# The last unit's stores: upper feature half through GpSimd's queue, lower half in four pieces of 64 KB

## The chip, the cores and the metric

The kernel runs on one core of one Trainium2 chip. The metric is the device time of one execution in microseconds (us). A core has TensorE (PE, matrix products), VectorE (DVE), ScalarE (ACT), GpSimd (POOL) and SyncE (SP); data enters and leaves through 16 DMA engines, which serve queues fed by SP, ACT and POOL.

## The reference

Attention whose keys and values are averaged over groups of 8 rows, followed by a mixer of two layers over tokens and two over channels. Cut to what matters:

```python
# q, k, v: (8 batches, 8 heads, 576 rows, 64)
k_p, v_p = mean of k and v over groups of 8 rows          # 72 rows each
attn_out = softmax(q @ k_p.T / 8) @ v_p
x  = attn_out, heads side by side                          # (8, 576, 512)
h  = relu(x.T @ w_tok1) @ w_tok2                           # over the 576 tokens
u  = x + h.T
out = u + relu(u @ w_ch1) @ w_ch2                          # 512 -> 1536 -> 512, float32
```

## The kernel before, in words

The work is ordered by hand: the whole body runs in a manual schedule. A head (`HEAD`) loads the first data, and then nine units follow, `unit(0)` to `unit(8)`, each with a plan (`PLANS`) of steps of later batches that are set between its own. Units 0 to 7 each take 512 of the 576 rows of one batch through the channel layers. The 64 rows that remain of every batch (the ninth row of each group of nine) are gathered in `u_tails` and `uT_tails`, and unit 8, the last one (`n == B`), takes the 512 rows of all eight batches at once.

From unit 2 on a unit is a `unit_fast`. It splits the second channel product (`GT`, hidden features, by `w_ch2`) into quarters and uses seven products of half size in the manner of Strassen instead of eight, with sums of the blocks in `area` and `area2`. `lo` and `hi` are the lower and the upper 256 of the 512 output features. PE's products are made by `product` (L777), which sums over `NH` = 6 blocks for each of two blocks `i` of 128 rows. The additions that complete an output are made on DVE by `plus` (L799). The outputs are two tiles, `oa` and `ob`, each of 128 partitions x 2 row blocks x 512 float32.

In units 2 to 7 `oa` and `ob` leave by `store` (L580): two issues on SP of 256 KB, one for each half of the partitions. In the last unit `oa` leaves in the same way. The products for `ob` come after it, the upper features first, each with a callback that is called after each row block `i`:

```python
store(n, 0, oa)
...
plus(ob[:, :, hi], x, s5, store_part(hi))
...
plus(ob[:, :, lo], x, u2lo, store_part(lo))
```

`store_part` (L810) does nothing after block 0. After block 1 it stores that feature half of `ob` for both blocks: partitions 0 to 63 by SP's queue and partitions 64 to 127 by ACT's, 128 KB each, as 128 rows of 1 KB. There are four such stores in all. `oa` has rows of 2 KB.

Nothing else is left to do at that point. The last work of POOL (L277, L145) lies near 177 us.

Of the kernel before, what the change touches and what calls it, by code (L numbers as in the profile page):

```python
# [61 lines left out]
def kernel(  # L62
# [14 lines left out]
    nc = tc.nc  # L77
# [4 lines left out]
    BP, BR = 64, S // 64  # L82
# [490 lines left out]
    def store(n, g, o):  # L573
        for half in range(2):
            rows = slice(half * BP, (half + 1) * BP)
            if n == B:
                dst = out.rearrange("(c h) (p r) n -> h p c r n", h=2, r=BR)[half][:, 2 * g:2 * g + 2, 8, :]
            else:
                dst = out[n].rearrange("(p r) n -> p r n", r=BR)[:, 4 * g + half:4 * g + half + 3:2, :]
            nc.sync.dma_start(out=dst, in_=o[rows])  # L580
# [26 lines left out]
    lo, hi = slice(0, 256), slice(256, 512)  # L607
# [30 lines left out]
    def keep(name):  # L638
        return outp.tile([P, 2, 256], FP32, name=name, bufs=1)
# [130 lines left out]
    def unit_fast(n, u):  # L770
        last = n == B
        late_steps = yield from (first_fast if n in GROUPS else first_stage)(n, u)

        def product(ps, a, w, start, after, split=False):
            for i in range(2):
                for m in range(NH):
                    nc.tensor.matmul(out=ps[i] if split else ps[:, i], lhsT=a(m)[:, i * P:(i + 1) * P], rhs=w(m),  # L777
                                     start=start and m == 0 and (i == 0 or split), stop=(m == NH - 1),
                                     skip_group_check=True)
                    if (i * NH + m) % 4 == 3 and (i, m) != (1, NH - 1):  # L780
                        yield
                if split:
                    after(i)
            if not split:
                after(slice(0, 2))
            yield

        def bank(split=False):
            if split:
                return [ps_two.tile([P, 2, 512], FP32, name="p2")[:, 0, 0:256] for _ in range(2)]  # L790
            return ps_one.tile([P, 2, 256], FP32, name="p1")

        def plus(out, ps, other, then=None):
            def go(i):
                src, dst = ps[i] if type(ps) is list else ps[:, i], out[:, i]
                if len(other.shape) == 4:
                    src, dst = (x.rearrange("p (a r) -> p a r", a=4) if type(i) is int else
                                x.rearrange("p c (a r) -> p c a r", a=4) for x in (src, dst))
                nc.vector.tensor_tensor(out=dst, in0=src, in1=other[:, i], op=ALU.add)  # L799
                if then is not None:  # L800
                    then(i)
            return go

        def store_part(cols):
            def go(i):
                if i == 0:
                    return
                for half in range(2):
                    dst = out.rearrange("(c h) (p r) n -> h p c r n", h=2, r=BR)[half]
                    (nc.scalar if half else nc.sync).dma_start(out=dst[:, 2:4, 8, cols],  # L810
                                                               in_=ob[half * BP:(half + 1) * BP, :, cols])
            return go

        SG, TW = fast["S"], fast["T"]

        def half_of(c, k):
            part = u["u"][:, c:c + 2]
            if n < BOUNCED or last:
                return part[:, :, 256 * k:256 * k + 256]
            return part.rearrange("p c (a k r) -> p c k a r", a=4, k=2)[:, :, k]  # L820

        u1lo, u1hi, u2lo, u2hi = half_of(0, 0), half_of(0, 1), half_of(2, 0), half_of(2, 1)
        oa, ob = (outp.tile([P, 2, DM], FP32, name="o") for _ in range(2))
        x, y = bank(last), bank()
        s1 = keep("s1")
        for i, _ in enumerate(product(x, lambda m: GT[:, m, lo], lambda m: w_ch2[:, m, lo], True,
                                      plus(s1, x, u1lo), last)):
            yield
            if late_steps and i < 2:
                late_steps[i]()  # L830
                yield
        yield from product(y, lambda m: GT[:, NH + m, lo], lambda m: w_ch2[:, NH + m, lo], True, plus(oa[:, :, lo], y, s1))
        z = bank()
        s5 = keep("s5")
        yield from product(z, lambda m: SG[:, 0, m], lambda m: TW[:, 0, m], True, plus(s5, z, u2hi))
        s2 = keep("s1")
        yield from product(x, lambda m: SG[:, 1, m], lambda m: TW[:, 1, m], False,
                           plus(s2, x, u1hi), last)
        if not last:
            w = bank()  # L840
            s4 = keep("s4")
            yield from product(w, lambda m: GT[:, NH + m, hi], lambda m: TW[:, 3, m], True, plus(s4, w, u2lo))
        yield from product(z, lambda m: SG[:, 3, m], lambda m: w_ch2[:, NH + m, hi], False, plus(oa[:, :, hi], z, s2))
        store(n, 0, oa)
        if last:
            yield from product(x, lambda m: SG[:, 2, m], lambda m: TW[:, 2, m], False,
                               plus(ob[:, :, hi], x, s5, store_part(hi)), True)
            yield from product(x, lambda m: GT[:, NH + m, hi], lambda m: TW[:, 3, m], False,
                               plus(ob[:, :, lo], x, u2lo, store_part(lo)), True)
        else:  # L850
            def finish(i):
                plus(ob[:, :, hi], x, s5)(i)
                plus(ob[:, :, lo], x, s4)(i)
            yield from product(x, lambda m: SG[:, 2, m], lambda m: TW[:, 2, m], False, finish)
            store(n, 1, ob)
# [112 lines left out]
```

## Time and profile before

| | |
|---|---|
| median of 3 runs | 271.18 us (270.85 to 271.25) |
| profiled execution, its own time | 271.6 us |
| its span, first to last instruction | 269.8 us |
| busy: PE, DVE, ACT, POOL | 96%, 77%, 45%, 42% of the span |
| moved by SP's queue (q1), ACT's (q10), POOL's (q0) | 12.39, 0.33, 22.11 MB |
| granted TensorE clock | 1.000 |

The span is what the trace shows; the time of an execution has 1.8 us more around it. An engine's busy share is a mean over stages, so for a change at the end of the kernel only the rows of the last stage count. A DMA issue's row on SP, ACT or POOL lasts as long as the issuing takes; the data moves later, and "landing" is counted from the start of the issue. The DMA share in a window is the mean busy share of the 16 engines; beside a window's edges it can read a little over 1.

### The profile page before, as it was taken

To read this page: it belongs to the slowest core of one execution; us is meant where nothing else is said; L and a number is where in the kernel's file an instruction comes from. 1 tells how busy PE (TensorE), PEld (TensorE's weight loads), DVE (VectorE), ACT (ScalarE), POOL (GpSimd) and SP (SyncE) were. 2 spreads that over 40 slices of the span, in tenths; PEclk is the share of its full clock that TensorE was granted. 3 is DMA by queue.
4 is the path that set the end of the run, shared out by engine and by line. 5 is a ranking of instruction groups with operands and counts; after the bars stand their busy time and mean duration, and the time that the engine had idled before them with its cause. 6 is when DMAs were issued, how large, how long until landed. Compare 5 with 4: busy or idle time off the path is not lost.

```text
span 269.8 us, 5432 instructions
## 1 busy us (share of the span) xinstructions
PE 259.5 (96%) x2173; PEld 171.7 (64%) x2200; DVE 206.8 (77%) x427; ACT 122.7 (45%) x207; POOL 113.4 (42%) x114
## 2 busy tenths in 40 slices
PE   8999999999999999999999999999999999999992
PEld 2776454545544645776587657864785688787781
DVE  4755573751798859996978798899799889997981
ACT  1375773047444353736563637264922632613600
POOL 5847749999995428636657242420000000000000
PEclk9999999999999999999999999999999999999999
DMA  7999999959969898998995997361506510404106
GB/s 184 190 194 205 204 212 204 180 126 190 153 132 140 154 159 118 146 169 168 155 141 83 156 213 87 39 164 40 119 0 147 149 18 21 137 2 116 41 2 157
DMA packets 42081, 35.17 MB, mean 130 GB/s; under 512 B 12040, under 2 KB 34408, under 8 KB 42056
## 3 DMA queue, kind: packets, MB, share of 16 engines
q0 software_dynamic: 30672, 22.11, 55.3%
q1 hardware_dynamic: 11056, 12.39, 17.2%
q10 hardware_dynamic: 328, 0.33, 0.5%
q8 instruction: 17, 0.28, 0.4%
q14 instruction: 8, 0.07, 0.1%
HBM read 36.90 MB, written 10.49 MB: 176 GB/s over the span
## 4 chain that ended last, share of the span: by engine, by line
PE 90%; DVE 5%; ACT 2%; issue 1%; DVEq 0%
PE p L777 24%; PE p L561 22%; PE p L695 9%; PE p L592 8%; PE p L453 6%; PE p L468 5%; PE p L357 4%; PE p L391 3%; PE p L862 3%; PE p L480 2%; PE p L323 1%; DVE area L614 1%; DVE u L470 1%; ACT ex L379 1%; ACT x L426 1%
## 5 line engine op out<-in xcount | busy, mean ns | idle before, releaser
L564 ACT ACTIVATE GT<-p 128x512 bf16<-128x512 f32 x76 | 44.5, 596 | 57.6 <-PE p L561 43.7
L561 PE MATMUL p<-uT,w_ch 128*128 128x512 bf16 x274 | 69.3, 380 | 0.9 <-issue 0.4
L561 PEld LDWEIGHTS <-w_ch 128*128 128x128 bf16 x304 | 32.4, 114 | 24.1 <-issue 1.7
L362 ACT ACTIVATE ex<-p 72x1024 bf16<-72x1024 f32 (+1 forms) x42 | 31.6, 804 | 27.5 <-PE p L357 27.3
L777 PEld LDWEIGHTS <-area 128*128 128x128 bf16 x336 | 31.9, 98 | 5.3 <-issue 1.3
L777 PE MATMUL p<-area,area 128*128 128x256 bf16 x252 | 30.8, 273 | 0.0
L145 POOL DMA_DIRECT2D kr<-in_k_dram x16 | 23.4, 1495 | 15.6 <-DMA kr<-in_k_dram 15.6
L145 POOL DMA_DIRECT2D vr<-in_v_dram x16 | 23.1, 1478 | 14.2 <-DMA vr<-in_v_dram 14.2
L470 DVE TENSOR_TENSOR u<-p,x 128x512 bf16<-128x512 f32 x32 | 21.1, 680 | 8.2 <-PE p L468 8.2
L777 PEld LDWEIGHTS <-GT 128*128 128x128 bf16 x252 | 24.2, 98 | 4.9 <-issue 0.6
L592 PE MATMUL p<-w_ch,GT 128*128 128x512 bf16 x92 | 23.6, 379 | 0.2
L777 PE MATMUL p<-w_ch,GT 128*128 128x256 bf16 x168 | 20.6, 273 | 0.1
L799 DVE TENSOR_TENSOR o<-p,s 128x512 f32<-128x512 f32 (+1 forms) x28 | 17.9, 662 | 3.2 <-PE p L777 3.1
L396 DVE TENSOR_TENSOR x<-p,den 128x512 bf16<-128x512 f32 x28 | 19.4, 691 | 1.0
L468 PE MATMUL p<-AT,w_tok 128*128 128x512 bf16 x62 | 17.3, 379 | 0.5 <-DVE u L470 0.5
L799 DVE TENSOR_TENSOR s<-p,u 128x512 f32<-128x512 f32 x24 | 16.2, 680 | 2.0 <-PE p L777 2.0
L395 DVE RECIPROCAL den<-p 128x8 f32<-128x8 f32 (+1 forms) x35 | 7.0, 201 | 11.3 <-PE p L391 10.9
L391 PEld LDWEIGHTS <-ex 72*128 72x128 bf16 x280 | 12.6, 98 | 3.9 <-DVE x L396 0.2
L592 PEld LDWEIGHTS <-GT 128*128 128x128 bf16 x96 | 8.8, 98 | 9.4 <-issue 0.4
L453 PE MATMUL p<-x,w_tok 128*128 128x512 bf16 x53 | 13.7, 379 | 0.2
L446 ACT ACTIVATE AT<-p 128x512 bf16<-128x512 f32 x14 | 8.4, 597 | 12.1 <-PE p L453 11.7
L391 PE MATMUL p<-vp,ex 72*128 72x65 bf16 x280 | 13.7, 194 | 0.0
(151 smaller groups left out, 448.8 us busy)
## 6 DMA issues: line engine op xcount, KB each, us to landing
out_dram<-o SPq DMA_DIRECT2D x34, 256.0 KB, 3.8
kr<-in_k_dram POOLq DMA_DIRECT2D x16, 288.0 KB, 7.4
vr<-in_v_dram POOLq DMA_DIRECT2D x16, 288.0 KB, 7.0
qb<-in_q_dram POOLq DMA_DIRECT2D x7, 576.0 KB, 10.1
kr<-in_k_dram POOLq DMA_DIRECT2D x3, 576.0 KB, 10.9
vr<-in_v_dram POOLq DMA_DIRECT2D x3, 576.0 KB, 12.4
w_ch<-in_moe_w_ch_dram POOLq DMA_DIRECT2D x6, 256.0 KB, 10.6
w_ch<-in_moe_w_ch_dram POOLq DMA_DIRECT2D x3, 512.0 KB, 13.1
```

Of the source, the lines that this page charges most:

```text
L145: nc.gpsimd.dma_start(out=pair_sums(b, key), in_=src[:, :, 2 * i * D:2 * (i + 1) * D], accum_op=ALU.add if i else ALU.bypass)
L362: nc.scalar.activation(out=exv[:, a, :, gs[0]:gs[-1] + 1, n0:n0 + n], func=AF.Exp, scale=scale, in_=pss[a][0:SP, :, 0:len(gs) * n].rearran ...
L391: nc.tensor.matmul(out=ps[:, h // 4, (h % 4) * (D + 1):(h % 4 + 1) * (D + 1)], lhsT=st["ex"][:, h * S + n0:h * S + n0 + P], rhs=st["vp"][: ...
L453: nc.tensor.matmul(out=ps, lhsT=w_tok1[:, c if c < 4 else 4 + par, m * P:(m + 1) * P], rhs=st["x"][:, c, :] if c < 4 else st["xt"], start= ...
L468: nc.tensor.matmul(out=ps, lhsT=w, rhs=a, start=(i == 0), stop=(i == len(mms) - 1))
L470: nc.vector.tensor_tensor(out=quads_of(dst, on), in0=plain_of(ps, on), in1=plain_of(x, on), op=ALU.add)
L561: nc.tensor.matmul(out=ps[m], lhsT=w_ch1[m // 4][:, kk, m % 4:512:4], rhs=moving(u)[kk], start=(kk == 0), stop=(kk == 3))
L564: nc.scalar.activation(out=GT[:, m, :], in_=ps[m], func=AF.Relu)
L592: nc.tensor.matmul(out=ps, lhsT=GT[:, m, c * P:(c + 1) * P], rhs=w_ch2[:, m, :], start=(m == 0), stop=(m == NM - 1))
L695: nc.tensor.matmul(out=ps[:, i], lhsT=w(i, k), rhs=mv(k), start=start and (i, k) == (0, 0), stop=stop and k == 1, skip_group_check=True)
L777: nc.tensor.matmul(out=ps[i] if split else ps[:, i], lhsT=a(m)[:, i * P:(i + 1) * P], rhs=w(m), start=start and m == 0 and (i == 0 or spli ...
L799: nc.vector.tensor_tensor(out=dst, in0=src, in1=other[:, i], op=ALU.add)
```

## The change

The callback now acts differently on the two feature halves. For the upper half (`cols == hi`) nothing happens after block 0, as before, and after block 1 both stores of 128 KB are issued from POOL instead of SP and ACT. For the lower half each block is stored as soon as it is complete, so there are two stores of 64 KB after block 0 and two after block 1, on SP and ACT. The bytes and the rows of 1 KB stay the same; L810 becomes L812.

```diff
         def store_part(cols):
             def go(i):
-                if i == 0:
+                if cols == hi and i == 0:
                     return
+                cs = slice(0, 2) if cols == hi else slice(i, i + 1)
                 for half in range(2):
                     dst = out.rearrange("(c h) (p r) n -> h p c r n", h=2, r=BR)[half]
-                    (nc.scalar if half else nc.sync).dma_start(out=dst[:, 2:4, 8, cols],
-                                                               in_=ob[half * BP:(half + 1) * BP, :, cols])
+                    eng = nc.gpsimd if cols == hi else (nc.sync, nc.scalar)[half]
+                    eng.dma_start(out=dst[:, 2 + cs.start:2 + cs.stop, 8, cols],
+                                  in_=ob[half * BP:(half + 1) * BP, cs, cols])
             return go
```

The order of the computing instructions on PE, DVE and ACT is the same in both kernels. POOL has two issues more ahead of its closing instructions.

## The prediction

> **What bounds the kernel now.** I read the chain of waits first, for the last 15 us of the span.
>
> ```profile
> 255.39 9.21 PE p L777 x84
> 264.60 0.02 issue
> 264.62 0.42 DVE o L799
> ```
>
> TensorE (PE) bounds this stage up to the last product, and the last VectorE (DVE) addition follows it at once, ending at 264.62 + 0.42 = 265.04. The span ends at 269.8: 4.8 us at the end have no computation in them. The change touches nothing ahead of 263.7, so everything lies in this tail. Next, the timeline from 261 us on, and what SyncE (SP) waits for in its last line (the columns there: total us, times, longest).
>
> ```profile
> 261.98 1.08 DVE L799 TENSOR_TENSOR o<-p,s 128x512 f32<-128x512 f32 x2 [0.89 <-PE p L777]
> 263.29 0.42 DVE L799 TENSOR_TENSOR o<-p,s 128x256 f32<-128x256 f32 x1 [0.23 <-PE p L777]
> 263.75 2.15 ACTq L810 DMA_DIRECT2D out_dram<-o  x2
> 263.97 0.42 DVE L799 TENSOR_TENSOR o<-p,u_tails 128x256 f32<-128x256 f32 x1 [0.25 <-PE p L777]
> 264.05 1.90 SPq L810 DMA_DIRECT2D out_dram<-o  x2
> 262.70 1.25 SPq L580 DMA_DIRECT2D out_dram<-o  x2
> SPq L963 <- DMA out_dram<-o: 2.4, 3, 1.6
> ```
>
> The upper half of `ob` is complete at 263.29 + 0.42 = 263.71, the first block of the lower half at 263.97 + 0.42 = 264.39, its second block at 265.04. Two stores of `oa` (256 KB each, L580) leave SP from 262.70. SP is still issuing them until 263.95, so its upper-half store starts at 264.05 and ScalarE's (ACT) at 263.75. After that SP waits for landings alone. The rows of L810 (ns min/median/max) and the last issues' landing:
>
> ```profile
> L810 ACTq DMA_DIRECT2D out_dram<-o x2: 738/778/818, 263.7 to 265.1; - x2
> L810 SPq DMA_DIRECT2D out_dram<-o x2: 630/750/870, 264.0 to 265.1; - x2
> DMA to landing us min/median/max: 3.3/3.5/3.7
> ```
>
> Both last issues start at 265.08 (SP's pair ends at 265.95 and the last took 870 ns; ACT's ends at 265.90 and took 818 ns). In the window of that second they land 3.3 us (ACT) and 3.7 us (SP) later, so the last landing is 265.08 + 3.7 = 268.8; another 1.0 us of closing semaphores makes 269.8. Last, what the DMA engines did meanwhile (the last two columns: busy share, GB/s):
>
> ```profile
> 264.00:265.00 1.00, 0.58 (x6) 0.28 (x3) 0.77 (x2) 0.00 (x0) 0.00 (x0) 1.00 0.99 197
> 265.00:266.00 1.00, 0.00 (x0) 0.00 (x0) 0.05 (x1) 0.00 (x0) 0.00 (x0) 1.00 0.96 257
> 265.60:265.80 0.20, 0.00 (x0) 0.00 (x0) 0.00 (x0) 0.00 (x0) 0.00 (x0) 1.00 1.04 317
> 266.40:266.60 0.20, 0.00 (x0) 0.00 (x0) 0.00 (x0) 0.00 (x0) 0.00 (x0) 1.00 0.71 159
> 266.60:266.80 0.20, 0.00 (x0) 0.00 (x0) 0.00 (x0) 0.00 (x0) 0.00 (x0) 1.00 0.77 164
> 267.00:268.00 1.00, 0.00 (x0) 0.00 (x0) 0.00 (x0) 0.00 (x0) 0.00 (x0) 1.00 1.01 285
> 268.30:268.40 0.10, 0.00 (x0) 0.00 (x0) 0.00 (x0) 0.00 (x0) 0.00 (x0) 1.00 0.20 62
> ```
>
> The tail stores 2 x 256 KB + 4 x 128 KB = 1.05 MB. Packets run from 263.9 to 268.36. So the end is set by the drain of the stores and not by the last addition alone. It is not an even drain: while `oa`'s first store runs by itself it moves 197 GB/s, then 317, then there is a dip at 266.4 to 266.8 with the engines 71 to 77% busy, then 285. The queues' packets in slices of 0.2 us say what the dip is: ACT's queue has its first packet of L810 at 265.95, 2.2 us after its issue at 263.75 (SP's first packet of `oa` came 1.2 us after issue), and SP's queue falls there from 31 packets a slice to 10. So the upper half arrives at the engines late, and one store's room is lost.
>
> **The change, part by part.** The profiled execution has a span of 269.8 and a time of 271.6, 1.8 more; the runs' median is 271.18. I carry differences from the span over to the median.
>
> *The upper half leaves SP and ACT.* Two issues go away (630 and 738 ns), with 128 rows of 1 KB each. On SP and ACT nothing stands behind them but the lower half's stores, so this makes both queues free at 264.39: SP has been idle since 263.95. By itself that is worth nothing in issue time, because today both queues are free at 264.68 and 264.49, before 265.04.
>
> *It enters GpSimd's (POOL) queue.* POOL did its last work at 178 us, and behind the two new issues stands only the closing barrier. Their first wait is for the addition ending at 263.71. The trace has no store from POOL, so its price is bounded by the loads:
>
> ```profile
> L180 POOL DMA_DIRECT2D w_tok<-in_moe_w_tok_dram x2: 547/654/762, 2.9 to 24.2; - x2
> L145 POOL DMA_DIRECT2D vr<-in_v_dram x16: 847/1400/2545, 44.5 to 171.0; - x16
> DMA to landing us min/median/max: 5.0/7.1/14.9
> ```
>
> A store here has 128 rows on 64 partitions; L180 has 64 rows, L145 has 576. I take 0.65 us, as the row of nearest shape, and keep 1.4 as the dear end. From 263.75 the two issues then end at 264.4 and 265.05 (dear: 265.15 and 266.55). The load of L145 at 170.96, met by no other traffic, ended its issue at 172.34 and had its first packets at about 172.95, 0.6 us behind. So the upper half's lower partitions reach the engines at about 265.0 and the upper ones at 265.65 (dear: 265.75 and 267.15). With the value taken, that is 0.3 to 1.0 us ahead of the 265.95 of ACT's queue today.
>
> The Trainium skill (DMA: Bandwidth & Descriptors, Latency and other measured facts) gives about 1 us to the first byte on GpSimd's path and 0.6 on the hardware path. By those figures alone the estimate is that the move starts the data 0.4 us later, a loss if the drain follows it; the trace shows both larger (about 2.0 at L145, 1.2 on SP, 2.2 on ACT behind `oa`), so the measured rows decide here.
>
> *The lower half in four stores of 64 KB.* Two issues are added: the first block's start at 264.43 on SP and ACT (ACT started 0.04 us after the addition today). Rows: 630 to 870 ns each, the high end when both queues issue together, so until about 265.25. The second block's issues wait for 265.04, so they start at 265.1 to 265.3 and end by 266.1. Their start is up to 0.2 later than today's 265.08, but they carry 128 KB between them where 256 KB are issued today. Total bytes and rows are unchanged; two more issues mean 32 more completion packets, which I cost at nothing (they are spread on 16 engines; without that cover, two per engine).
>
> *The sum.* Up to 265.2 the trace shows 119 packets of 2 KB, 0.24 MB; 0.805 MB remain. Today they need 268.36 - 265.2 = 3.16 us, a mean of 255 GB/s. With a third queue filled from 265.0, and the first half of the lower columns issued 0.65 us earlier than any of it is today, I expect the dip to go. At 317 GB/s (the slice at 265.6) the rest takes 2.54 us, to 267.74: a gain of 0.62. At 285 (the second at 267) it takes 2.82, to 268.02: 0.34. At the best slice (323 at 267.0) 2.49: 0.67. The last block cannot be what holds this up: from 265.3 with ACT's 3.3 us it would land at 268.6, though that 3.3 covers double the bytes and a full drain. Without that shrinking the gain would end at 0.2, which is the weak end. I take 0.6: span 269.2, its own time 271.0, a median of 270.58, about **270.6**. That case reaches from a gain of 0.2 to one of 1.0: 0.67 by the best slice, 0.1 for two queues instead of one between 265.0 and 265.2, and 0.2 if a half-size last store also shortens the 0.4 us from its last packet to its landing.
>
> **Rivals.** *A: the dip is filled*, the forecast, 270.6. For it: 71 to 77% busy engines in the dip, and ACT's 2.2 us to the first packet.
>
> *B: the drain stays as long as it is*, 271.2 (270.8 to 271.5). The engines are marked 0.96 to 1.01 busy in the three other full seconds from 264 to 268, and bytes and rows are the same. If a filled dip only lowers the rate later (with two queues the share at 266.0 is 0.97 at 261 GB/s), the last packet stays at 268.36. That the change does nothing for the drain is this case too. The Trainium skill (DMA: Bandwidth & Descriptors, Issuing engines are not separate DMA queues) states this: DMAs of all issuers interleave on the same 16 engines, and more issuers save only issue time. The full shares in the trace agree with it; the dip does not.
>
> *C: GpSimd's second store lands last*, slower. Its price: landings of POOL's issues in the trace are 4.1 us at the least (the early loads of 32 and 256 KB) and 5.0 at the least on L145. With a start at 264.4 it lands at 268.5 by the one and at 269.9 by a plain landing of 5.5 (the load at 163.71); the dear issue time would make it 270.65. Against today's 268.8 that is -0.3, +1.1 and +1.85 us. It decides from a landing of 4.4 us on. Against it: the 5.5 us belong to 288 KB in 576 short rows, whose packets alone ran over 3 us; for it: POOL has been idle for 85 us, no store has gone that way, and the rotation over three queues may serve its short rows last. Its time: 272.3, reaching from 271.8 to 273.
>
> **How the numbers follow.** About 0.2% (0.54 us) is what a measurement of this kernel can tell from no change. A has 0.60, B 0.14, C 0.26. Some 0.7 of A lie beyond 0.54, since 0.62 and 0.67 come from rates that the tail itself shows: faster 0.42. The rest of A, 0.18, and B make 0.32 within 0.2%. C makes 0.26 slower. The range runs from 270.2, which takes in nearly all of A, over B, to 272.1, a little under C's middle: about 0.18 stay out. A's own range is 270.2 to 271.0.
>
> **What would show it.** If right: POOL shows two issues from 263.75 at 0.55 to 0.8 us each, its queue has packets by 265.3, the slice at 266.4 to 266.8 is over 0.9 busy, the last packet is at about 267.8, and the last landing belongs to a 64 KB store of SP or ACT at about 268.2. B: the same issues, but the last packet stays within 0.2 us of 268.36. C: POOL's queue has the last packets, after 268.5, and its second store lands 4.4 us or more after its issue. Wrong altogether: the additions of L799 move, or the closing steps after the last landing take other than 1.0 us.

## The result and the profile after

| | before | after |
|---|---|---|
| median of 22 runs each | 271.06 us | 272.19 us |
| profiled execution, its own time | 271.6 us | 272.25 us |
| its span | 269.8 us | 270.5 us |

The ratio is 1.0044, with a 95% interval of 1.0028 to 1.0060: by the medians the change costs 1.13 us. Two runs of the experiments, one of e9 (449.5 us) and one of e11 (686.8 us), stand far above all others and are left out of the ratios. The additions of L799 in the changed kernel end at 264.71, in the kernel before at 265.05. A difference of 0.34 us ahead of the stores says nothing: in the 17 profiled executions, whose computing instructions are the same, this moment lies between 264.10 and 265.94. So I count the tail from the end of the last addition (T) and not from the span's start. In these two executions it grew from 4.76 to 5.78 us, by 1.02, and two further profiled executions gave 4.72 and 5.77. The tail repeats to 0.04 us where the ratio of 12 runs is good to 0.15 to 0.24% (0.4 to 0.65 us). Most verdicts below rest on it, and so on one profiled execution of each kernel.

The changed kernel's timeline from 262 us shows when the stores leave (a row is start, duration, engine and line):

```profile
262.36 1.25 SPq L580 DMA_DIRECT2D out_dram<-o  x2
262.95 0.42 DVE L799 TENSOR_TENSOR o<-p,s 128x256 f32<-128x256 f32 x1 [0.23 <-PE p L777]
263.68 1.32 POOL L812 DMA_DIRECT2D out_dram<-o  x2 [81.38 <-DVE o L799]
264.08 1.30 SPq L812 DMA_DIRECT2D out_dram<-o  x2
264.09 1.42 ACTq L812 DMA_DIRECT2D out_dram<-o  x2
264.28 0.42 DVE L799 TENSOR_TENSOR o<-p,u_tails 128x256 f32<-128x256 f32 x1 [0.23 <-PE p L777]
```

SP and ACT begin 0.03 us after the lower half's first block, as was foreseen. POOL begins at 263.68, 0.31 us after the upper half is complete (262.95 + 0.42 = 263.37); in e4 and e11 too it begins 0.30 us after the addition that it waits for. All six issues are over at 265.5. The DMA engines in the microseconds that follow (the last two columns: busy share, GB/s) are another matter:

```profile
265.00:266.00 1.00, 0.00 (x0) 0.00 (x0) 0.00 (x0) 0.00 (x0) 0.00 (x0) 1.00 0.90 272
266.00:267.00 1.00, 0.00 (x0) 0.00 (x0) 0.00 (x0) 0.00 (x0) 0.00 (x0) 1.00 0.79 224
267.00:268.00 1.00, 0.00 (x0) 0.00 (x0) 0.00 (x0) 0.00 (x0) 0.00 (x0) 1.00 0.77 246
268.00:269.00 1.00, 0.00 (x0) 0.00 (x0) 0.00 (x0) 0.00 (x0) 0.00 (x0) 0.86 0.10 34
```

The kernel before in the window with its dip (what the prediction calls a second is such a window of 1 us):

```profile
266.00:267.00 1.00, 0.00 (x0) 0.00 (x0) 0.00 (x0) 0.00 (x0) 0.00 (x0) 1.00 0.88 215
```

The dip is still there, and it is longer: 0.79 and 0.77 of the engines where the windows at 266 and 267 had 0.88 and 1.01 before. The last packet is at T + 3.64 (268.35). What follows it is told by the changed kernel's DMA issues (KB each, median us to landing) and by its last line's rows, the closing instructions (ns min/median/max, first and last start; L963 before, L965 now):

```profile
out_dram<-o SPq DMA_DIRECT2D x2, 64.0 KB, 4.2
out_dram<-o ACTq DMA_DIRECT2D x2, 64.0 KB, 4.4
L965 POOLq DRAIN  x3: 51/97/5577, 264.1 to 270.2; - x3
L965 POOLq EVENT_SEMAPHORE  x4: 17/17/17, 269.7 to 270.4; - x4
L965 SPq DRAIN  x3: 7/7/13, 269.5 to 270.0; - x3
```

The stores of 64 KB land 4.2 and 4.4 us after their issue, where the last two stores of 128 KB took 3.3 and 3.7. POOL's longest DRAIN begins at 264.1 and ends 5.58 us later, at 269.7. The closing order was the same in both kernels: SP waits for each store's landing in a fixed row of waits of about 65 ns each and drains (its first drain at 269.0 before, 269.5 now), POOL sets the first semaphore of the end barrier (269.1 before, 269.7 now), and 0.75 us later the span ends. Taken apart, in us after T:

| | last packet | last landing | SP's DRAIN | POOL's semaphore | end |
|---|---|---|---|---|---|
| before | 3.37 | 3.71 | 3.92 | 4.01 | 4.76 |
| after | 3.64 | 4.42 | 4.78 | 5.03 | 5.78 |

**0.71 us** is the later last landing (0.27 from a later last packet, 0.44 because the landing follows it after 0.78 instead of 0.34). **0.15** is SP's row of waits: the store that lands last is now one of ACT's, whose wait stands earlier in the row, so more waits follow it (0.36 from landing to DRAIN instead of 0.21). **0.16** is POOL's DRAIN, which holds the barrier 0.26 us after SP's instead of 0.09.

### The profile page after: what moved, and what is told of

It reads as the page before. It is cut to its first block, busy times and chain, and to the rows that moved or that the text cites. A ratio compares the mean times of both kernels' runs of the same rounds, so it can differ in the third digit from the quotient of the medians.

```text
span 270.5 us, 5434 instructions
## 1 busy us (share of the span) xinstructions
PE 258.8 (96%) x2173; PEld 171.5 (63%) x2200; DVE 205.7 (76%) x427; ACT 122.8 (45%) x207; POOL 115.4 (43%) x116
## 4 chain that ended last, share of the span: by engine, by line
PE 84%; DVE 6%; DMA 2%; ACT 2%; POOL 2%; issue 1%; POOLq 0%; DVEq 0%
PE p L777 23%; PE p L561 22%; PE p L695 9%; PE p L592 8%; PE p L468 6%; PE p L453 5%; PE p L357 4%; PE p L391 3%; DMA vr<-in_v_dram 2%; PE p L480 2%; PE p L323 1%; DVE area L614 1%; DVE u L470 1%; ACT ex L379 1%; DVE kr L664 1%
## 5 line engine op out<-in xcount | busy, mean ns | idle before, releaser
L812 POOL DMA_DIRECT2D out_dram<-o x2 | 1.3, 666 | 81.4 <-DVE o L799 81.4
L799 DVE TENSOR_TENSOR o<-p,s 128x512 f32<-128x512 f32 (+1 forms) x28 | 18.0, 663 | 3.2 <-PE p L777 3.1
L799 DVE TENSOR_TENSOR s<-p,u 128x512 f32<-128x512 f32 x24 | 16.2, 681 | 1.2 <-PE p L777 1.2
```

## The experiments

Diffs are against the changed kernel where they name `cs`, else against the kernel before. In us after T, unless a row says otherwise, the runs gave:

| kernel | last packet | last landing | SP's DRAIN | end | ratio to before, 95% |
|---|---|---|---|---|---|
| before, again (e8) | 3.34 | 3.67 | 3.88 | 4.72 | 1.0005 (0.9989 to 1.0020) |
| after, again (e7) | 3.65 | 4.42 | 4.78 | 5.77 | 1.0032 (1.0017 to 1.0047) |
| e1 upper half on POOL, no split | 3.39 | 3.73 | 4.60 | 5.45 | 1.0013 (0.9997 to 1.0028) |
| e2 split, nothing on POOL | 3.33 | 4.01 | 4.10 | 4.94 | 1.0018 (0.9997 to 1.0038) |
| e3 `oa` by SP and ACT | 3.15 | 3.61 | 3.90 | 4.74 | 1.0012 (0.9992 to 1.0033) |
| e4 `oa`'s lower part on POOL | 3.58 | 3.91 | 4.68 | 5.52 | 1.0014 (0.9995 to 1.0034) |
| e5 upper half all on ACT | 3.33 | 3.67 | 4.38 | 5.22 | 1.0015 (0.9993 to 1.0038) |
| e6 as e1, one SP issue more | 3.38 | 3.72 | 4.50 | 5.34 | 1.0020 (1.0003 to 1.0038) |
| e9 as e1, three more | 3.51 | 4.11 | 4.32 | 5.17 | 1.0009 (0.9987 to 1.0031) |
| e10 upper half left out | 2.17 | 2.64 | 3.10 | 3.94 | 0.9982 (0.9962 to 1.0002) |
| e11 lower block 0 on POOL | 3.46 | 4.09 | 4.33 | 5.28 | 1.0023 (0.9999 to 1.0047) |
| e12 e11 and e3 together | 3.29 | 3.79 | 4.09 | 5.00 | 1.0030 (1.0012 to 1.0048) |
| e13 lower block 0 left out | 3.11 | 3.67 | 4.55 | 5.39 | one execution |
| e17 half of the upper half on POOL | 3.25 | 3.75 | 4.02 | 4.86 | one execution |
| e18 split issued late | 3.67 | 4.43 | 4.79 | 5.79 | one execution |

**The two parts by themselves.** e1 sends the upper half through POOL and leaves the lower half whole; e2 splits the lower half and uses POOL for nothing.

```diff
 # e1_hi_on_pool, against before
-                    (nc.scalar if half else nc.sync).dma_start(out=dst[:, 2:4, 8, cols],
-                                                               in_=ob[half * BP:(half + 1) * BP, :, cols])
+                    eng = nc.gpsimd if cols == hi else (nc.sync, nc.scalar)[half]
+                    eng.dma_start(out=dst[:, 2:4, 8, cols], in_=ob[half * BP:(half + 1) * BP, :, cols])
 # e2_lo_split, against after
-                    eng = nc.gpsimd if cols == hi else (nc.sync, nc.scalar)[half]
-                    eng.dma_start(out=dst[:, 2 + cs.start:2 + cs.stop, 8, cols],
-                                  in_=ob[half * BP:(half + 1) * BP, cs, cols])
+                    (nc.scalar if half else nc.sync).dma_start(out=dst[:, 2 + cs.start:2 + cs.stop, 8, cols],
+                                                               in_=ob[half * BP:(half + 1) * BP, cs, cols])
```

> Only the first part of the change: the upper half's two stores go through GpSimd's queue, the lower half leaves by two stores of 128 KB after its second block, as before. Theory P (GpSimd's queue is the cost: data 2.2 us after the issue, a late landing and a long closing DRAIN on GpSimd): 0.8 to 1.3 us slower than before, as slow as the whole change, with GpSimd's DRAIN ending last. Theory S (the split is the cost: two more issues, whose stores land 4.2 to 4.5 us after issue instead of 3.3 to 3.7): within 0.3 us of before.

> Only the second part: the lower half in four stores of 64 KB, all stores on SyncE and ScalarE. Theory P: between no change and 0.4 us faster, since the first block leaves 0.65 us earlier. Theory S: 0.8 to 1.3 us slower than before, with the last landing 4.2 us or more after its issue.

Neither part makes the whole. With POOL alone the last landing is where it was (3.73), yet the end comes 0.69 us later. With the split alone the last landing is 0.30 later, and the steps after it take 0.92 instead of 1.05, since its wait is the last of the row. The ratios alone decide for neither theory. The timeline of e2 shows a late issue:

```profile
263.53 2.85 ACTq L811 DMA_DIRECT2D out_dram<-o  x3
263.83 2.76 SPq L811 DMA_DIRECT2D out_dram<-o  x3
```

Three issues on SP take 2.76 us: that of the lower half's first block took 1168 ns, from T - 0.27 to T + 0.90, so the second block's store began at T + 1.02. But the drain did not suffer by it: the last packet is at 3.33, before at 3.37. The whole delay lies between the last packet and the landing, 0.69 us instead of 0.34. The two landings, 0.02 and 0.30 us later when alone, make 0.71 together.

**`oa` over two queues.** The prediction took the late start of ACT's data behind `oa` for room that another queue could fill. e3 gives `oa`'s upper partitions to ACT, e4 its lower partitions to POOL.

```diff
 # e3_oa_two_queues, against before, in store (L580)
-            nc.sync.dma_start(out=dst, in_=o[rows])
+            (nc.scalar if n == B and half else nc.sync).dma_start(out=dst, in_=o[rows])
 # e4_oa_low_on_pool, the same line
+            (nc.gpsimd if n == B and not half else nc.sync).dma_start(out=dst, in_=o[rows])
```

> The kernel before, with the last unit's oa stored by SyncE (partitions 0 to 63) and ScalarE (64 to 127) instead of SyncE alone; nothing else differs. If the drain's rate sets the end, and its first 1.3 us run at 197 GB/s because only the lower 64 partitions are read then, both halves together start at about 315 GB/s and the end comes 0.3 to 0.5 us sooner. If the end is set by the last issues and their landing (3.3 to 3.7 us after 265.04), no change (within 0.2 us). Neither theory P nor S speaks of it.

> The kernel before, with one store of oa (partitions 0 to 63, 256 KB) on GpSimd's queue, issued 1.3 us earlier than the upper half's could be. Theory P in the form that GpSimd's late landing costs: its store lands by 267.5, ahead of the last ones, and the time is within 0.3 us of before, or a little faster. Theory P in the form that any GpSimd store in the tail makes GpSimd's closing DRAIN long: the DRAIN ends at 269.5 or later whatever the landing, and the time is 0.5 us or more above before. Theory S: no change.

e3 gained nothing (4.74). Its timeline has the first two stores of `oa` issued at the same moment:

```profile
263.21 0.59 SPq L580 DMA_DIRECT2D out_dram<-o  x1
263.21 0.72 ACTq L580 DMA_DIRECT2D out_dram<-o  x1
```

Its queues in 264.45 to 265.75 and, after the dots, in 265.75 to 267.0 (packets, MB, share of the engines) show them one after the other:

```profile
q1 hardware_dynamic: 120, 0.25, 97.7%
...
q10 hardware_dynamic: 139, 0.26, 77.3%
q1 hardware_dynamic: 87, 0.08, 21.5%
```

For the first 1.3 us the engines are taken by SP's store alone, and ACT's queue (q10) has its first packet at T + 0.28, when SP's are through. The Trainium skill (DMA: Bandwidth & Descriptors, Queues, rings and completion order) says that each engine takes its queues in turn and drains a whole packet, typically about 9 to 17 descriptors (each names one piece of data to move), from one before it switches. These rows agree with that: by an estimate that spreads a store's 128 rows evenly, each of the 16 engines has 8 of them and a completion to do, no more than one such packet (the profile counts each row of the store as a packet of its own). In e4 POOL's store of `oa` has its first packet at T + 0.30, at the same place. So the 2.2 us to a first packet behind `oa` are a place in line, and another issuer gets the same place.

Two things more can be read here. e3 has no dip:

```profile
266.45:267.25 0.80, 0.00 (x0) 0.00 (x0) 0.00 (x0) 0.00 (x0) 0.00 (x0) 1.00 0.98 265
```

Its last packet comes 0.22 sooner than before, its last landing 0.10 sooner, and its end at the same time. And in e4 POOL's DRAIN ends at T + 2.91, 0.91 after its store has landed and long before SP's: a store on POOL does not hold the end by itself.

**What holds the end in e1.** In e1 nothing lands after T + 3.73, and SP's DRAIN is at 4.60. Either POOL's closing steps hold it or SP's own do. e5 has no store on POOL but the same number of issues on SP as e1; e6 and e9 are e1 with one and three SP issues more, made by cutting stores of `oa` in unit 7 in two.

```diff
 # e5_hi_both_on_act, against before
-                    (nc.scalar if half else nc.sync).dma_start(out=dst[:, 2:4, 8, cols],
+                    (nc.scalar if half or cols == hi else nc.sync).dma_start(out=dst[:, 2:4, 8, cols],
 # e6_pool_shifted: e1, and in store; e9_pool_shifted3: the same for (g, half) != (1, 1)
+            if n == B - 1 and g == 0 and half == 0:
+                nc.sync.dma_start(out=dst[:, 0:1], in_=o[rows, 0:1])
+                nc.sync.dma_start(out=dst[:, 1:2], in_=o[rows, 1:2])
+                continue
             nc.sync.dma_start(out=dst, in_=o[rows])
```

> The kernel before, with both upper-half stores on ScalarE, so that SyncE issues as many stores at the end as it does with the upper half on GpSimd, and GpSimd none. Two theories on the 0.47 us that SyncE loses between two of its closing waits whose landings are long past (profiles of the first and the fourth experiment: 3.92 to 4.39 us after the last addition). Theory G, it comes with GpSimd's stores: no such gap here, end of span 4.7 to 5.0 us after the last addition. Theory I, it belongs to SyncE's own instruction stream (a stall after a certain number of instructions, hidden where a landing is waited for at that place): the gap is here too, and the end comes 5.2 to 5.5 us after the last addition.

> The first experiment (upper half on GpSimd, lower half unsplit), with one store of unit 7 on SyncE cut in two, 18 us ahead of the end: one more issue in SyncE's stream, nothing else in the tail. Theory G: the gap of 0.47 us stays, end 5.3 to 5.5 us after the last addition. Theory I: the place of the stall moves by an issue to a wait that is held up by a landing anyway, the gap goes, and the end comes about 4.9 to 5.0 us after the last addition.

> The first experiment (upper half on GpSimd, lower half unsplit) with three stores of unit 7 on SyncE cut in two, 18 us ahead of the end: three more issues in SyncE's stream. The gap of 0.47 us has moved by one closing wait for one issue, from after the last landing to just behind it. If it belongs to SyncE's stream, three issues put it ahead of the wait for the last landing (at 3.7 us after the last addition), where it is covered: the end comes 4.85 to 5.05 us after the last addition instead of 5.34 to 5.45. If it belongs to GpSimd's stores, it stays behind the landing and the end at 5.3 to 5.5.

It is SP's, though not by e6's end, which lies in theory G's band. e5 has the late end without POOL, and its last landing is at 3.67. The closing waits of e5 (268.4 to 268.8 and 269.0 to 269.3; none lies between) and those of e1 (268.15 to 268.45 and 268.45 to 269.2) show a hole in the row:

```profile
L963 SPq EVENT_SEMAPHORE  x1: 27/27/27, 268.6 to 268.6; - x1
...
L963 SPq EVENT_SEMAPHORE  x3: 28/28/28, 269.1 to 269.2; - x3
```

```profile
L963 SPq EVENT_SEMAPHORE  x3: 28/28/28, 268.2 to 268.4; - x3
...
L963 SPq EVENT_SEMAPHORE  x3: 28/28/28, 268.9 to 269.0; - x3
L963 POOLq DRAIN  x1: 4574/4574/4574, 263.9 to 263.9; - x1
```

Between two of SP's waits 0.47 us pass although all that they wait for has landed: from 3.69 to 4.16 in e5, 3.92 to 4.39 in e1, 3.93 to 4.40 in e4, 3.74 to 4.21 in e6. One SP issue more moves the hole one wait ahead, still behind the last landing; in e9, with three more, it lies at 0.81 to 1.29, ahead of the landings at the end, and costs nothing (SP's DRAIN 0.21 after the last landing, as before). In all eight profiles that show it (e1, e4, e5, e6, e9, e10, e13, e17) it stands before the 80th of SP's instructions in the trace. So it is a stall at a place in SP's instruction stream. In before and after it is hidden behind the landings. POOL's DRAIN in e1 ends at 263.9 + 4.574 = 268.5 (T + 4.0), well ahead of SP's: with an ordinary step of 0.08 in place of the hole e1 would end at about 5.05, and e1's 5.45 says little against POOL.

With the hole out of the way e9 ends at 5.17, between the bands of the two theories, and not at about 4.8, because its last landing came 0.4 later (4.11). For that the runs show no reason. So it is the place of the hole that decides between the theories, and not e9's end.

**What the stores of the upper half do to the others.** e10 leaves the upper half out, so its output lacks these 256 KB; e13 leaves out the lower half's first block, 128 KB.

```diff
 # e10_hi_left_out, against after
-                if cols == hi and i == 0:
+                if cols == hi:
                     return
 # e13_lo0_left_out, the same line of after
+                if i == 0:
                     return
```

> The changed kernel with the upper half of the last two row blocks not stored at all (256 KB less; that part of the output is missing); the lower half leaves in four stores of 64 KB as in the change. Theory M (GpSimd's data, in packets of 4 KB on the same engines, hold the 64 KB stores up): the last landing falls from 4.42 to 3.5 us or less after the last addition, and the stores' last packets from 3.6 to 2.9 or less. Theory S (the splitting itself makes them late): the last landing stays at 4.0 us or more.

> The changed kernel without the stores of the lower half's first block (128 KB less; that part of the output is missing). Theory C (the early block shares the engines with GpSimd's packets and makes all of them late): the last landing falls by more than its bytes cost at 285 GB/s (0.46 us), from 4.42 to 3.6 us or less. Theory N (the 64 KB stores behind the last addition are late by themselves beside GpSimd's): 3.9 us or more.

Without the upper half the same four stores of 64 KB land much sooner (e10's DMA issues, KB each and median us to landing):

```profile
out_dram<-o SPq DMA_DIRECT2D x2, 64.0 KB, 2.6
out_dram<-o ACTq DMA_DIRECT2D x2, 64.0 KB, 2.7
```

The last landing is 1.78 us earlier than in the changed kernel, and 256 KB at the 285 GB/s of the window at 267 before are 0.92. Of the 1.78 us, 1.47 are an earlier last packet and the rest a shorter way from packet to landing. So the split is not slow as such: the upper half cost these stores about twice the time of its bytes. Leaving out 128 KB of the lower half (e13) brought 0.75, where its bytes are worth 0.46. That lies between what the two theories said and decides nothing.

**The same split and bytes, other queues.** e17 leaves the split as it is and gives half of the upper half back to ACT. e18 was to issue the four small stores after the second block.

```diff
 # e17_half_on_pool, against after
-                    eng = nc.gpsimd if cols == hi else (nc.sync, nc.scalar)[half]
+                    eng = nc.gpsimd if cols == hi and half == 0 else (nc.sync, nc.scalar)[half]
 # e18_split_late, against after
-                if cols == hi and i == 0:
+                if i == 0:
                     return
-                cs = slice(0, 2) if cols == hi else slice(i, i + 1)
-                for half in range(2):
+                for cs, half in ([(slice(0, 2), h) for h in range(2)] if cols == hi else
+                                 [(slice(c, c + 1), h) for c in range(2) for h in range(2)]):
```

> The changed kernel with half of the upper half on GpSimd (partitions 0 to 63) and half on ScalarE (64 to 127). If the amount on GpSimd's queue counts, the last landing lies between the split without GpSimd (4.01) and the change (4.42), about 4.2 us; if any store of GpSimd beside the split does it, 4.4 us or more. ScalarE has three issues and may be late by itself, as SyncE was in the split alone.

> The changed kernel with the lower half's four stores of 64 KB all issued after the second block, so that nothing of it leaves early. Theory C: without the early block GpSimd's stores are through by 3.1 us as in the first experiment, and the last landing is 3.7 to 4.2 us, earlier than the change's 4.42 although its last issue is 0.6 us later. Theory N: 4.4 us or more, later by that issue.

e17 undoes nearly all of the loss: the last landing is at 3.75, sooner than either theory had it, and the end at 4.86 (one execution). The windows from T + 0.9 to T + 1.7 (last two columns: share, GB/s) tell the difference. The changed kernel:

```profile
265.60:266.40 0.80, 0.00 (x0) 0.00 (x0) 0.00 (x0) 0.00 (x0) 0.00 (x0) 1.00 0.72 196
```

The kernel before:

```profile
265.94:266.74 0.80, 0.00 (x0) 0.00 (x0) 0.00 (x0) 0.00 (x0) 0.00 (x0) 1.00 0.93 227
```

e1:

```profile
265.37:266.17 0.80, 0.00 (x0) 0.00 (x0) 0.00 (x0) 0.00 (x0) 0.00 (x0) 1.00 0.83 236
```

e17:

```profile
265.97:266.77 0.80, 0.00 (x0) 0.00 (x0) 0.00 (x0) 0.00 (x0) 0.00 (x0) 1.00 1.01 279
```

In the changed kernel `oa`'s last packets are at T + 1.40. POOL's first come at T + 1.15 and are few, ACT's first at T + 1.35. In e17 ACT has a store of 128 KB in line at this point and the dip is gone.

e18 is a miss: the edit moved the lines to another callback, but each queue still had the same issues in the same order, and they left when the data was there. The first block's stores again left at T - 0.6, and it became the changed kernel, its tail within 0.02 us.

**Roles exchanged.** e11 puts the lower half's first block on POOL and the upper half on SP and ACT; e12 adds e3's edit.

```diff
 # e11_lo0_on_pool, against after
-                    eng = nc.gpsimd if cols == hi else (nc.sync, nc.scalar)[half]
+                    eng = nc.gpsimd if cols == lo and i == 0 else (nc.sync, nc.scalar)[half]
```

> A version between the two: the upper half on SyncE and ScalarE as before, the lower half's first block (two stores of 64 KB) on GpSimd, its second on SyncE and ScalarE. SyncE and ScalarE issue as many stores as before, the last of them half as large, and GpSimd carries half as much as in the change. If GpSimd's bytes and the waiting of SyncE behind its own issues were what hurt, the last landing is 3.3 to 3.7 us after the last addition and the tail 4.5 to 4.8 us (before: 4.72 to 4.76); if any split or any GpSimd store hurts, the tail is 4.9 us or more.

> The version with the lower half's first block on GpSimd, and oa stored by SyncE and ScalarE together as in the third experiment (whose last packets ended 0.2 us sooner than before's). If the two add up, the last landing is 3.2 to 3.5 us after the last addition and the tail 4.4 to 4.7 us; otherwise 4.7 or more. A time within 0.2% of before either way.

Tails of 5.28 and 5.00, both outside the hopeful bands: no version with the whole output has a tail clearly shorter than the kernel before. In both, POOL's DRAIN ends after SP's, as in the changed kernel. e12 missed its time as well: 0.30% above before (0.12 to 0.48), about 0.8 us, where its tail is only 0.24 us longer; the runs show no reason for the rest.

**The controls.**

> The changed kernel again, on the chip and with the runs of the kernel before of this call. Its tail was 5.78 us from the last addition to the end against 4.76 before. If that is the change's and not this one execution's, the tail is again 5.5 to 6.0 us, the last landing (of a 64 KB store) 4.2 to 4.6 us after the last addition, GpSimd's DRAIN ends about 0.9 us after GpSimd's own last landing, and the time is 0.3 to 0.6% above before.

> The kernel before, unchanged, as a control: it shows what a ratio of 12 runs and the tail of one profile are worth. Ratio within 0.15% of 1; tail 4.6 to 4.9 us from the last addition to the end, last landing 3.6 to 3.9 us.

The changed kernel is slower again (1.0032), and the kernel before against itself gives no difference (1.0005).

## Why the prediction was wrong, step by step

The forecast was a gain of 0.6 us and the result is a loss of about 1. From the forecast tail of 4.14 (4.76 less 0.62) to the measured 5.78 there are 1.64 us, in three terms.

*"I expect the dip to go"* (0.89 us: last packet at 3.64 where 2.75 was worked out). This step failed first. It supposed POOL's data at the engines at 265.0, which is T - 0.05 in the profile before. The first packet came at T + 1.15 (265.85 in the changed kernel's profile): POOL's issue began 0.27 us later than supposed, the issues took 684 and 647 ns, nearly as taken, and the first packet followed the first issue's end after 1.5 us instead of 0.6. The 0.6 us behind the end were read from a load "met by no other traffic", while this store stood behind `oa`, as ACT's did before, also with 2.2. e3 and e4 show that a second queue's store waits until the one issued ahead of it is through or nearly so; a third queue therefore could not bring its data in ahead of `oa`. The Trainium skill (DMA: Bandwidth & Descriptors, Issuing engines are not separate DMA queues) says that more issuers save only issue time; that POOL, idle for 81 us before its issue, brought the data no sooner agrees with it. That section was put beside rival B, which kept the drain at its length; but the drain became longer, 3.64 against 3.37. With the upper half away from SP and ACT less stood in line there when `oa` ended, and e17, which gives half of it back to ACT, has neither the dip nor the loss. But the dip is not the whole of it: e1's smaller dip (0.83) cost next to nothing (3.39). And the prediction put the price of a dip too high. Where the dip did go, the last packet came 0.12 (e17) and 0.22 us (e3) sooner than before and not 0.62, the last landing 0.04 later and 0.10 sooner, and neither tail got shorter by more than the 0.04 to which it repeats.

*"32 more completion packets, which I cost at nothing"*, and the half-size store that "shortens the 0.4 us from its last packet to its landing" (0.44 us: it grew from 0.34 to 0.78). The direction was wrong. By the table it is 0.47 or more in every kernel with the split (e2, e10 to e13, e17, e18), and 0.33 or 0.34 in the kernels without it (before, e1, e4, e5, e6), but for e3 (0.46) and e9 (0.60). The trace says where it builds up. Each store ends with 16 completion packets of 4 bytes and has landed with the last of its 16 landing signals: 96 of each in the kernel before, 128 in the changed one. Counted in order, a signal follows its packet by 0.32 to 0.37 us all the way in the kernel before. In the changed kernel this holds for the first 49 (0.31 to 0.41); then the distance grows, not quite evenly, to 0.77. The last five landings there follow each other by 0.18 to 0.19 us (3.67, 3.86, 4.04, 4.23 and 4.42), on three different queues, and in e7 and e18 they do so again by 0.18 to 0.20. That reads as a backlog that runs through all the last stores, POOL's too, and not as a delay of the last one alone. The 32 more packets are a candidate for its cause, but no run shows it: e10 and e13 have 96, as before, and still end with 0.47 and 0.56. The Trainium skill (DMA: Bandwidth & Descriptors, Latency and other measured facts) lets the fixed cost of a DMA shrink with a lighter load on memory; e10, with the fewest bytes, has 0.47, more than the kernel before, so that by itself does not explain it.

*"Another 1.0 us of closing semaphores"* (0.31: 1.36 in the changed kernel, 1.05 before). It was taken as a constant, and "the closing steps after the last landing take other than 1.0 us" stood among the signs of being wrong altogether. It depends on which queue's store lands last (0.15) and on POOL's DRAIN (0.16). "Behind the two new issues stands only the closing barrier", the prediction said of POOL, and priced them by their landing alone; in the eleven profiles with stores on POOL the DRAIN ended 0.91 to 0.95 us after POOL's last landing (in the changed kernel at 4.99, after 4.04).

Rival C had the side and the size (+1.1, measured +1.13 in the medians) by another mechanism. POOL's second store landed 4.4 us after its issue, at C's deciding point, at T + 4.04, and POOL's queue did not have the last packets. The last landing was a 64 KB store of ACT, as A had said, at T + 4.42.

Right were POOL's issue times, the start of each store of SP and ACT, and that the computing instructions do not change. The issues of the 64 KB stores took 494 to 763 ns where 630 to 870 were taken. Of the rise of 1.02 us the runs show 0.16 as POOL's DRAIN and 0.15 as the order of waits. The 0.27 of the later last packet needs both parts (3.39 in e1, 3.33 in e2) and all 256 KB on POOL (3.25 in e17). The 0.44 behind it is the growing distance of the landings from their packets, most of which the split brings by itself (0.69 in e2); what makes the landings fall behind stays open.

## What to carry to other kernels

Where the last stores stand in line behind others at the DMA engines, as here behind `oa`, another issuer for some of them need not bring their bytes forward, and taking them out of the queues that follow can leave the engines short when the store ahead ends; look at what is in line at each moment, not at when each issue starts. Price a store at the very end by everything up to the last instruction: its packets, its landing, the place of its wait in the closing row, and the drain of the engine that issued it. Where single runs differ by more than the effect, the stretch from the last computing instruction to the end repeats far better than the whole time.

## What the runs showed of the hardware

- POOL's closing DRAIN ends 0.91 to 0.95 us after POOL's own last store has landed, and the end barrier waits for it. It cost something where it ended after SP's (after, e11, e12) and nothing in e1, e4, e6, e9, e13 and e17.
- POOL's issue begins 0.30 us after the addition that it waits for (after, e1, e4, e11), SP's and ACT's 0.03.
- Once in SP's row of closing waits 0.47 to 0.48 us pass between two waits instead of 0.06 to 0.09, always before the 80th of its instructions. It costs only where no landing is awaited there. What it is the runs do not show.
- Landing signals can fall behind their completion packets: from 0.33 us to 0.77 with eight stores at the end, the last five landings 0.18 to 0.19 us apart.
- Two stores of 256 KB issued on SP and ACT at the same moment did not share the engines: the second had its first packet 1.4 us after the first's, when the first was through (e3).
- Through POOL's queue 256 KB in rows of 1 KB are 96 packets, 32 of them completions, so 4 KB each; SP and ACT send one packet for each row. The changed kernel's queues in 262 to 269 us (packets, MB, share of the engines):

```profile
q0 software_dynamic: 96, 0.26, 12.4%
q10 hardware_dynamic: 160, 0.13, 5.7%
```
